# Renumbering the rows of a partition-wise DFT so that row and weight transfers get other partitions, and reloading a weight from a laid-out copy

## The chip, the cores and the metric

The kernel runs on one core of one Trainium2 chip. The metric is the device time of that core for one execution, in microseconds (us). A profile records one execution; its span, from first to last instruction, is about 2 us shorter than the device time of the same execution. Engines: PE is TensorE, PEld its weight loads, DVE is VectorE, ACT is ScalarE, POOL is GpSimd, and SP or SPq is SyncE and its queue, which issues nearly all DMAs of this kernel. A "stage" below begins with the first matmul of a group of matmuls.

The runs are labelled fast or slow. On one core that label rests only on the distance to the fastest run of the same kernel (1.5%).

## The reference

The kernel computes the output and all gradients of one block: a spectral filter with a residual, then a token MLP with a residual, both behind a LayerNorm, in bf16.

```python
# S = 2048, D = 448, Df = 225, F = 1792; all inputs bf16
def A(x, w_r, w_i):                               # spectral filter
    X = rfft2(x.astype(float32), axes=(-2, -1))   # [S, 225] complex
    X = X * (w_r + 1j * w_i)                      # w_r, w_i: [2048, 225]
    return irfft2(X, s=(S, D)).astype(bfloat16)
def B(x, w1, b1, w2, b2):                         # token MLP
    u = gelu(einsum("bsd,sf->bdf", layernorm(x), w1) + b1)
    return (einsum("bdf,fs->bds", u, w2) + b2).transpose(0, 2, 1)
h = x + A(layernorm(x), w_r, w_i)
y = h + B(layernorm(h), w1, b1, w2, b2)
# outputs: y and the gradients of x, w_r, w_i, w1, b1, w2, b2 for grad_out   (cut)
```

## The kernel before

The FFT over S = 2048 is written as matrix products with generated sine and cosine matrices, in two steps of 128 and 16. Between the steps a matmul result (one value of `s1`, 128 partitions) becomes eight partitions of 16 rows in another tile, which a DMA does. I call these the *row DMAs*: 16 per direction in the forward pass and again in the backward pass, each moving 128 packets of 904 bytes.

```python
def s1_stage(s1, ab):
    p1 = ps_ff(); p1v = ...
    nc.tensor.matmul(p1v, lhsT=Rm[:], rhs=ab, start=True, stop=True)
    cs = r452_ring.next(); evac(out=cs, in_=p1v)
    nc.sync.dma_start(out=D2[s1:P:16, :, 0:2, :], in_=cs)      # partitions s1, s1+16, ...
def s2_inv(g, y):
    ...                                                        # two matmuls with UTt, VTt
    ab = r452_ring.next(); evac(out=ab, in_=pv)
    nc.sync.dma_start(out=D3[g:P:16, :, :, :], in_=ab)
```

The spectral weight is brought into the matching order by 18 DMAs, each onto 16 neighbouring partitions with 15 or 16 rows (in two of them one row) of 450 bytes per partition. The same helper runs three times: the load for the forward pass, the same load again for the backward pass (into a buffer that holds MLP data until then), and the store of the weight's gradients.

```python
def w_io(Wv, dr, di, store, eng):
    for c_, d in ((0, dr), (1, di)):
        def go(part, g0, g1, d_ap):
            sb = Wv[part[0]:part[1], g0:g1, c_, 0:DF]
            ...                                   # eng.dma_start, in or out
        for f in range(4):
            go((16 * f, 16 * f + 16), 0, 16, d.rearrange("(a r) k -> a r k", r=P)[:, 16 * f:16 * f + 16, :])
        ...                                       # four mirrored groups, and one row group
...
w_io(W_view_F, A_w_r, A_w_i, False, nc.sync)      # before the s1 loop
...
nc.sync.dma_start_transpose(out=du_t..., in_=rD[...])
gp_.memset(W_view_B[:, :, :, DF:KW], 0.0)
w_io(W_view_B, A_w_r, A_w_i, False, nc.sync)      # backward, in rD
...
w_io(W_view_B, out_2, out_3, True, nc.sync)       # after the backward s2 stage
```

The second step of the FFT (the *s2 stage*) stores the forward spectrum for the backward pass and keeps two buffers for it (`X_ring`). Behind it stand two loads of 1 MB, the first chunks of w1; the second of them goes to a region shared with `D2`. And matmuls that do not depend on the stage at hand fill gaps of PE: in the forward s2 stage and before it, the MLP product of `grad_out` with w2, which needs *w2 transposes* (DMA transposes into `rE`); in the backward stages, the gradients of w2 (from `rE`) and w1 (from `rB`), both through transposes into `rst`.

```python
def fwd_mult(c2, xc):
    nc.sync.dma_start(out=xspec_d[:, 2 * c2:2 * c2 + 2, :, :], in_=xc)
    return w_mult(c2, xc, W_view_F, False)
s2_stage(fwd_mult, N_FILL_F[3], N_FILL_F[4])
w1c_ring = ring(r2, 0, 2, NT, 256)
w1cs = [load_w1c(0), load_w1c(1)]                 # 1 MB each
```

PE's instructions keep the order of the program (the kernel sets `manual_schedule` for PE alone). The compiler's scheduler orders all other engines, the SyncE queue included.

Of the kernel before, what the change touches and what calls it, by code (L numbers as in the profile page):

```python
# [16 lines left out]
P = 128  # L17
# [42 lines left out]
def kernel(  # L60
# [84 lines left out]
    cols = mem.tile([P, 48], F32, name="cols")  # L145
    _ci = [0]

    def col(n=1):
        i = _ci[0]
        _ci[0] += n  # L150
        assert _ci[0] <= 48
        return cols[:, i:i + n]
# [21 lines left out]
    smr = mem.tile([16, 2, P], BF16, name="smr")  # L174
    smc = mem.tile([P, 2, 16], BF16, name="smc")

    xspec_d = dram.tile([P, NG, 2, KW], BF16, name="xspec_d")
# [19 lines left out]
    gtail = mem.tile([16, P], BF16, name="gtail")  # L197
    gp_.memset(gtail[:], 0.0)
# [57 lines left out]
    def gen_R():  # L256
        ge = ftmp(2560, P)
        t = ftmp(2688, P)
        q = ftmp(2816, P)
        fr = ftmp(2944, P)  # L260
        ve.tensor_scalar(out=ge, in0=krow[:, 0:P], scalar1=65.0, scalar2=None, op0=ALU.is_ge)
        ve.scalar_tensor_tensor(out=fr, in0=ge, scalar=-64.0, in1=krow[:, 0:P], op0=ALU.mult, op1=ALU.add)
        ve.tensor_scalar(out=t, in0=fr, scalar1=pcol, scalar2=32.0, op0=ALU.mult, op1=ALU.add)
        ve.scalar_tensor_tensor(out=t, in0=ge, scalar=32.0, in1=t, op0=ALU.mult, op1=ALU.add)
        center(ve, q, t, 128)
        sc.activation(out=Rm[:], in_=q, func=ACT.Sin, scale=s128)
        gec = col()
        fc = col()
        oc = col()
        ve.tensor_scalar(out=gec, in0=pcol, scalar1=65.0, scalar2=None, op0=ALU.is_ge)  # L270
        ve.scalar_tensor_tensor(out=fc, in0=gec, scalar=-64.0, in1=pcol, op0=ALU.mult, op1=ALU.add)
        ve.tensor_scalar(out=oc, in0=gec, scalar1=32.0, scalar2=32.0, op0=ALU.mult, op1=ALU.add)
        t2 = ftmp(3072, P)
        q2 = ftmp(3200, P)
        ve.tensor_scalar(out=t2, in0=krow[:, 0:P], scalar1=fc, scalar2=oc, op0=ALU.mult, op1=ALU.add)
        center(ve, q2, t2, 128)
        sc.activation(out=RTm[:], in_=q2, func=ACT.Sin, scale=s128)

    c64, f2lo, lo, msk = col(), col(), col(), col(4)

    def gen_pidx(eng):
        w = col()
        floor_div(eng, c64, pcol, 64)
        floor_div(eng, w, pcol, 16)
        eng.tensor_scalar(out=lo, in0=w, scalar1=-16.0, scalar2=None, op0=ALU.mult)
        eng.tensor_tensor(out=lo, in0=lo, in1=pcol, op=ALU.add)
        eng.tensor_scalar(out=f2lo, in0=c64, scalar1=-4.0, scalar2=None, op0=ALU.mult)
        eng.tensor_tensor(out=f2lo, in0=f2lo, in1=w, op=ALU.add)
        for j in range(4):
            eng.tensor_scalar(out=msk[:, j:j + 1], in0=f2lo, scalar1=float(j), scalar2=None,  # L290
                              op0=ALU.is_equal)

    comp_ring = ring(rO, 0, 4, 32, 16)

    def expand(dst, q):
        d = dst[:].rearrange("p g (c f l) -> p (g c) f l", c=2, f=4)
        comp = comp_ring.next()
        sc.activation(out=comp, in_=q.rearrange("p g c l -> p (g c) l"), func=ACT.Sin, scale=s2048)
        for j in range(4):
            gp_.tensor_scalar(out=d[:, :, j, :], in0=comp, scalar1=msk[:, j:j + 1], scalar2=None, op0=ALU.mult)  # L300
        gp_.memset(dst[0:16, 0, 64:80], 0.0)
        gp_.memset(dst[64:80, 0, 0:16], 0.0)

    def gen_UV(eng):
        base = ftmp(512, 16, 2, 16)
        iota(base[:, :, 0, :], [[1, 16], [128, 16]])
        gp_.iota(base[:, :, 1, :], pattern=[[1, 16], [-128, 16]], base=1920, channel_multiplier=0,
                 allow_small_or_imprecise_dtypes=True)
        slf = col()
        eng.tensor_tensor(out=slf, in0=lo, in1=f2lo, op=ALU.mult)  # L310
        eng.tensor_scalar(out=slf, in0=slf, scalar1=16.0, scalar2=512.0, op0=ALU.mult, op1=ALU.add)
        ou, ov0, ov1, pu, pv, l64 = col(), col(), col(), col(), col(), col()
        eng.tensor_scalar(out=ou, in0=c64, scalar1=1536.0, scalar2=None, op0=ALU.mult)
        eng.tensor_tensor(out=ou, in0=ou, in1=slf, op=ALU.add)
        eng.tensor_scalar(out=ov0, in0=c64, scalar1=-512.0, scalar2=512.0, op0=ALU.mult, op1=ALU.add)
        eng.tensor_tensor(out=ov0, in0=ov0, in1=slf, op=ALU.add)
        eng.tensor_scalar(out=ov1, in0=ov0, scalar1=1024.0, scalar2=None, op0=ALU.add)
        eng.tensor_scalar(out=l64, in0=lo, scalar1=64.0, scalar2=None, op0=ALU.mult)
        for pt, o, k0 in ((pu, ou, -1536.0), (pv, ov1, -512.0)):
            eng.tensor_scalar(out=pt, in0=l64, scalar1=k0, scalar2=None, op0=ALU.add)  # L320
            eng.tensor_tensor(out=pt, in0=pt, in1=o, op=ALU.add)
        for dst, o0, o1, pt in ((Ut, ou, ou, pu), (Vt, ov0, ov1, pv)):
            t = ftmp(1024 if dst is Ut else 2048, 16, 2, 16)
            q = ftmp(1536 if dst is Ut else 2560, 16, 2, 16)
            for s_, o in ((0, o0), (1, o1)):
                eng.tensor_scalar(out=t[:, :, s_, :], in0=base[:, :, s_, :], scalar1=lo, scalar2=o,
                                  op0=ALU.mult, op1=ALU.add)
            eng.tensor_scalar(out=t[64:80, 0, 1, :], in0=base[64:80, 0, 0, :], scalar1=lo[64:80], scalar2=pt[64:80],
                              op0=ALU.mult, op1=ALU.add)
            center(eng, q, t, 2048)  # L330
            expand(dst, q)

    def gen_UVT(eng):
# [5 lines left out]
        v, v64 = col(), col()  # L339
        eng.tensor_scalar(out=v64, in0=lo, scalar1=128.0, scalar2=64.0, op0=ALU.mult, op1=ALU.add)  # L340
        eng.tensor_scalar(out=v, in0=lo, scalar1=-2.0, scalar2=15.0, op0=ALU.mult, op1=ALU.add)
        eng.tensor_tensor(out=v, in0=v, in1=c64, op=ALU.mult)
        eng.tensor_tensor(out=v, in0=v, in1=lo, op=ALU.add)
        eng.tensor_scalar(out=v, in0=v, scalar1=8.0, scalar2=None, op0=ALU.mult)
        eng.tensor_tensor(out=v, in0=v, in1=f2lo, op=ALU.add)
        eng.tensor_scalar(out=v, in0=v, scalar1=16.0, scalar2=None, op0=ALU.mult)
        t0 = ftmp(1024, 16, 2, 16)
        eng.tensor_scalar(out=t0, in0=srow, scalar1=v, scalar2=None, op0=ALU.mult)
        eng.tensor_tensor(out=base, in0=base, in1=t0, op=ALU.add)
        oc0, oc1 = col(), col()  # L350
        eng.tensor_scalar(out=oc0, in0=c64, scalar1=1024.0, scalar2=1024.0, op0=ALU.mult, op1=ALU.add)
        eng.tensor_scalar(out=oc1, in0=c64, scalar1=1024.0, scalar2=512.0, op0=ALU.mult, op1=ALU.add)
        for dst, o0, o1, pc in ((UTt, 512.0, 2048.0, 512.0), (VTt, oc0, oc1, 1024.0)):
            t = ftmp(1024 if dst is UTt else 2048, 16, 2, 16)
            q = ftmp(1536 if dst is UTt else 2560, 16, 2, 16)
            for c_, o in ((0, o0), (1, o1)):
                eng.tensor_scalar(out=t[:, :, c_, :], in0=base[:, :, c_, :], scalar1=o, scalar2=None, op0=ALU.add)
            eng.tensor_scalar(out=t[64:80, 0, 1, :], in0=srow[64:80, 0, 1, :], scalar1=v64[64:80], scalar2=pc,
                              op0=ALU.mult, op1=ALU.add)
            center(eng, q, t, 2048)  # L360
            expand(dst, q)
# [25 lines left out]
    gen_R()  # L387
# [5 lines left out]
    def w_io(Wv, dr, di, store, eng):  # L393
        for c_, d in ((0, dr), (1, di)):
            def go(part, g0, g1, d_ap):
                sb = Wv[part[0]:part[1], g0:g1, c_, 0:DF]
# [4 lines left out]
            for f in range(4):  # L401
                go((16 * f, 16 * f + 16), 0, 16,
                   d.rearrange("(a r) k -> a r k", r=P)[:, 16 * f:16 * f + 16, :])
            for f in range(4):
                g0 = 1 if f == 0 else 0
                first = P - 16 * f - g0
                go((64 + 16 * f, 80 + 16 * f), g0, 16,
                   bass.AP(d.tensor, d.offset + first * DF, [[P * DF, 16], [-DF, 16 - g0], [1, DF]]))
            go((64, 80), 0, 1, d.rearrange("(a r) k -> a r k", r=P)[:, 64:65, :])
# [14 lines left out]
    def resh_eng():  # L424
        _ei[0] += 1
        return nc.sync

# [25 lines left out]
    def s1_stage(s1, ab):  # L453
# [5 lines left out]
        nc.sync.dma_start(out=D2[s1:P:16, :, 0:2, :], in_=cs)  # L459
# [39 lines left out]
    def s2_inv(g, y):  # L499
# [6 lines left out]
        nc.sync.dma_start(out=D3[g:P:16, :, :, :], in_=ab)  # L506
# [83 lines left out]
    gen_pidx(ve)  # L590
    gen_UV(ve)
# [4 lines left out]
    w_io(W_view_F, A_w_r, A_w_i, False, nc.sync)  # L596
    fill(N_FILL_F[0])
    ab = None
    for s1 in range(NT):
# [4 lines left out]
        fill(N_FILL_F[1])  # L604
        if s1 % 2 == 1 and s1 // 2 + 3 < NT // 2:
            prep_x(s1 // 2 + 3)
        if s1 == 3:
            gen_UVT(ve)
# [8 lines left out]

    s2_stage(fwd_mult, N_FILL_F[3], N_FILL_F[4])
# [35 lines left out]
    gp_.memset(smr[:], 0.0)  # L654
# [68 lines left out]
    nc.sync.dma_start_transpose(out=goT[:, 3, S - 16:S], in_=gtail[:])  # L723
# [95 lines left out]
    gp_.memset(W_view_B[:, :, :, DF:KW], 0.0)  # L819
    w_io(W_view_B, A_w_r, A_w_i, False, nc.sync)  # L820
# [76 lines left out]
    w_io(W_view_B, out_2, out_3, True, nc.sync)  # L897
# [41 lines left out]
```

## Time and profile before

The kernel took 502.93 us (median of 3 runs, 500.79 to 504.31); the profiled span is 500.2 us.

| reading | before | view |
|---|---|---|
| PE, VectorE, ScalarE busy | 75%, 52%, 47% | page, busy shares |
| time of the DMA queue's packets over 16 engines | 81.9% of the span | page, DMA queues |
| PE's wait at the first w2-gradient matmul | 17.2 us | waits |
| PE's wait for w2 transposes at the start | 21.6 us | waits |
| DMA share, 20 to 80 us | 1.04 | stretches |

The page of the kernel before says which engines are busy (busy us, share of the span, instructions), how full the DMA engines are (packets, MB, share of 16 engines), and who holds the chain of waits that ended last:

```profile
PE 376.9 (75%) x1920; PEld 189.9 (38%) x1920; DVE 261.1 (52%) x709; ACT 235.1 (47%) x478; POOL 39.5 (8%) x50
...
q1 hardware_dynamic: 177320, 87.50, 81.9%
...
PE 40%; DMA 32%; DVE 17%; ACT 5%; SPq 4%; issue 3%; DVEq 0%; POOLq 0%; POOL 0%; ACTq 0%
```

No engine is busy throughout, so what is saved in a stage must be read from that stage. The view of PE's waits (engine, line, tile, releaser: us in all, times, longest us) has these among its largest in the kernel before:

```profile
PE ps_mm L567 <- DMA rE<-in_B_w_dram: 21.6, 3, 8.6
...
PE ps_mm L865 <- DMA rst<-rE: 17.2, 1, 17.2
...
PE ps_mm L880 <- DMA rst<-rB: 6.2, 2, 4.2
PE ps_ff L514 <- DMA r_73<-r_78: 5.5, 2, 3.7
```

L567 is the fill product behind the w2 transposes; L865 and L880 are the gradients of w2 and w1; L514 is the first matmul after the forward s2 stage, which needs the last row DMA. The reason for the 17.2 us stands in the timeline of the SyncE queue in the kernel before (start, time spent issuing, operation, out<-in, number):

```profile
324.20 1.26 SPq L437 DMA_TRANSPOSE rT<-rF  x1
...
326.48 4.70 SPq L400 DMA_DIRECT2D rD<-in_A_w_r_dram  x9
332.25 9.55 SPq L400 DMA_DIRECT2D rD<-in_A_w_i_dram  x9
342.88 0.62 SPq L459 DMA_DIRECT2D r_72<-r_78  x1
344.13 1.22 SPq L851 DMA_TRANSPOSE rst<-rE  x1
```

Eighteen issues of the second weight load hold the queue from 326.5 to 341.8 us, and the row DMA and the transpose that PE needs come behind them. What that does to PE is in the table by stretches of the kernel before (start:end, length, busy us and instructions of PE, PEld, DVE, ACT and POOL, granted TensorE clock, DMA share, GB/s; the DMA share adds up overlapping packets and may pass 1):

```profile
20.00:80.00 60.00, 40.07 (x197) 21.40 (x197) 38.62 (x119) 27.62 (x53) 30.76 (x28) 0.83 1.04 150
320.00:340.00 20.00, 9.36 (x35) 4.07 (x33) 0.00 (x0) 6.50 (x13) 0.25 (x1) 0.74 1.20 154
340.00:360.00 20.00, 8.67 (x28) 3.41 (x29) 1.31 (x4) 2.15 (x4) 0.00 (x0) 0.58 1.23 149
```

In all three the DMA engines are full (shares of 1.04, 1.20 and 1.23), though they move only 149 to 154 GB/s.

### The profile page before, as it was taken

The numbers are of one execution on the slowest core, as the hardware profiler recorded it, in microseconds if no ns is written. First come the engines' busy times: TensorE is split into PE (matmuls) and PEld (weight loads), VectorE is DVE, ScalarE is ACT, GpSimd is POOL, SyncE is SP. The second block draws the span as 40 slices with busy tenths as digits, with TensorE's granted clock in tenths as the row PEclk, the third lists the DMA queues.
The fourth block names the chain that finished last, engine by engine and source line by source line (L and its number), as shares of the span: only waits on it lengthen the run. The fifth ranks groups of instructions, "written<-read, shape, count | busy, mean of one in ns | idle before, by whom it ended". The sixth has DMA issues, their size and how long they took to land.

```text
span 500.2 us, 6019 instructions
## 1 busy us (share of the span) xinstructions
PE 376.9 (75%) x1920; PEld 189.9 (38%) x1920; DVE 261.1 (52%) x709; ACT 235.1 (47%) x478; POOL 39.5 (8%) x50
## 2 busy tenths in 40 slices
PE   2553865967798999639789999750899996969960
PEld 0221532433453445314344555320344443535530
DVE  9988362652494888602127867200137770235664
ACT  0622753653374545102222444730378784758771
POOL 6007960000000000000000000000000000000000
PEclk9975988899898999959999999965799998889995
DMA  9999799498975753785659999899956887976641
GB/s 234 209 156 158 149 152 168 119 221 173 269 215 188 196 171 85 159 220 160 191 164 169 202 168 192 163 140 94 194 188 190 215 202 181 166 197 183 205 166 55
DMA packets 177351, 87.87 MB, mean 176 GB/s; under 512 B 123433, under 2 KB 172585, under 8 KB 177193
## 3 DMA queue, kind: packets, MB, share of 16 engines
q1 hardware_dynamic: 177320, 87.50, 81.9%
q8 instruction: 15, 0.25, 0.2%
q14 instruction: 16, 0.12, 0.1%
HBM read 29.40 MB, written 23.89 MB: 107 GB/s over the span
## 4 chain that ended last, share of the span: by engine, by line
PE 40%; DMA 32%; DVE 17%; ACT 5%; SPq 4%; issue 3%; DVEq 0%; POOLq 0%; POOL 0%; ACTq 0%
DMA out_dram<-r_81 9%; PE ps_mm L865 8%; PE ps_mm L687 7%; PE ps_mm L809 5%; PE ps_mm L567 5%; PE ps_mm L880 4%; DVE stats L547 3%; PE ps_mm L732 3%; DMA r_73<-r_78 3%; DMA r_73<-in_B_w_dram 2%; DMA rC<-rD 2%; DMA rD<-in_A_w_i_dram 2%; DMA rE<-in_B_w_dram 2%; DMA xspec_d<-rS 2%; DVE r_81 L783 2%
## 5 line engine op out<-in xcount | busy, mean ns | idle before, releaser
L567 PE MATMUL ps_mm<-rC,rE 128*128 128x448 bf16 x224 | 62.5, 414 | 29.1 <-DMA rE<-in_B_w_dram 21.6
L865 PE MATMUL ps_mm<-rG,rst 112*128 112x512 bf16 x224 | 56.2, 400 | 17.9 <-DMA rst<-rE 17.2
L880 PE MATMUL ps_mm<-rC,rst 112*128 112x512 bf16 (+1 forms) x256 | 55.9, 367 | 6.9 <-DMA rst<-rB 6.2
L732 PE MATMUL ps_mm<-rE,rS 128*128 128x448 bf16 x224 | 44.9, 361 | 17.7 <-DMA rS<-in_B_w_dram 17.7
L687 PE MATMUL ps_mm<-rB,r_72 128*128 128x448 bf16 x224 | 45.0, 362 | 2.9 <-DVE rB L646 1.9
L567 PEld LDWEIGHTS <-rE 128*128 128x128 bf16 x224 | 24.3, 111 | 54.8 <-DMA rE<-in_B_w_dram 22.5
L809 PE MATMUL ps_mm<-rD,r_73 128*128 128x448 bf16 x224 | 43.7, 352 | 1.5 <-DMA r_73<-in_B_w_dram 1.5
L868 ACT CAST rO<-ps_mm 128x512 bf16<-128x512 f32 x56 | 31.7, 596 | 26.8 <-PE ps_mm L865 26.5
L865 PEld LDWEIGHTS <-rst 112*128 112x128 bf16 x224 | 22.8, 102 | 46.9 <-DMA rst<-rE 17.7
L732 PEld LDWEIGHTS <-rS 128*128 128x128 bf16 x224 | 21.9, 100 | 40.5 <-DMA rS<-in_B_w_dram 19.9
L883 ACT CAST rO<-ps_mm 128x512 bf16<-128x512 f32 (+1 forms) x60 | 30.1, 541 | 13.7 <-PE ps_mm L880 13.4
L880 PEld LDWEIGHTS <-rst 112*128 112x128 bf16 x256 | 25.0, 101 | 30.2 <-DMA rst<-rB 6.8
L744 ACT ACTIVATE r_81<-rC 128x448 bf16<-128x448 bf16 x16 | 9.2, 576 | 48.8 <-DVE r_81 L739 38.1
L687 PEld LDWEIGHTS <-r_72 128*128 128x128 bf16 x224 | 22.2, 100 | 25.5 <-issue 5.0
L528 PE MATMUL ps_ff<-csI,rAT 113*128 113x448 bf16 x128 | 30.7, 365 | 0.6 <-ACT rAT L517 0.5
L809 PEld LDWEIGHTS <-r_73 128*128 128x128 bf16 x224 | 21.6, 98 | 24.0 <-DMA r_73<-in_B_w_dram 2.6
L739 DVE SCALAR_TENSOR_TENSOR r_81<-ps_mm,b2col,r_81 128x448 bf16<-128x448 f32 x16 | 10.8, 682 | 37.9 <-PE ps_mm L732 37.8
L463 DVE TENSOR_SCALAR r_72<-r_72 128x904 bf16<-128x904 bf16 x8 | 2.6, 390 | 50.3 <-DMA r_72<-r_78 50.3
L450 ACT CAST r_78<-ps_ff 128x452 bf16<-128x452 f32 x32 | 17.2, 541 | 22.5 <-PE ps_ff L447 22.4
L517 ACT CAST rAT<-ps_ff 113x512 bf16<-113x512 f32 x32 | 18.4, 584 | 14.1 <-PE ps_ff L514 14.0
L477 ACT CAST rS<-ps_ff 128x452 bf16<-128x452 f32 x30 | 16.2, 542 | 15.2 <-PE ps_ff L476 10.6
L777 ACT ACTIVATE r_81<-ps_mm 128x448 bf16<-128x448 f32 x16 | 8.7, 543 | 29.8 <-PE ps_mm L809 28.7
(192 smaller groups left out, 599.6 us busy)
## 6 DMA issues: line engine op xcount, KB each, us to landing
r_72<-in_B_w_dram SPq DMA_DIRECT2D x7, 1024.0 KB
rS<-in_B_w_dram SPq DMA_DIRECT2D x8, 896.0 KB
out_dram<-rO SPq DMA_DIRECT2D x14, 512.0 KB
out_dram<-rO SPq DMA_DIRECT2D x16, 448.0 KB
r_72<-r_78 SPq DMA_DIRECT2D x32, 113.0 KB
r_73<-r_78 SPq DMA_DIRECT2D x32, 113.0 KB
out_dram<-r_81 SPq DMA_DIRECT2D x32, 112.0 KB
xspec_d<-rS SPq DMA_DIRECT2D x8, 226.0 KB
```

The costliest lines, as they stand in the source:

```text
L450: sc.copy(out=ab, in_=pv)
L477: evac(out=xc[:, i, :, :], in_=pv)
L517: sc.copy(out=aT[0:KC].rearrange("p a b -> p (a b)"), in_=pa[0:KC, :])
L528: nc.tensor.matmul(py[:, 0:D], lhsT=aT[0:KC, i, :], rhs=csI[0:KC, i // 2, i % 2, :], start=(i == 0), stop=(i == 3))
L567: nc.tensor.matmul(pg[:, 0:D], lhsT=wT[:, t, :], rhs=go_tp[:, t, :], start=(t == 0), stop=(t == NT - 1))
L687: nc.tensor.matmul(pu[:, 0:D], lhsT=w1c[:, t, jj * P:(jj + 1) * P], rhs=hln[:, t, :, :], start=(t == 0), stop=(t == NT - 1))
L732: nc.tensor.matmul(py[:, 0:D], lhsT=w2cs[t // 2][:, j, (t % 2) * P:(t % 2 + 1) * P], rhs=g_[:, j, :, :], start=(j == 0), stop=(j == NFB - 1))
L809: nc.tensor.matmul(pdh[:, 0:D], lhsT=wT[:, j, :], rhs=du[:, j, :, :], start=(j == 0), stop=(j == NFB - 1))
L865: nc.tensor.matmul(pw[:], lhsT=gt[0:DC, k, :], rhs=goT[0:DC, k, c * 512:(c + 1) * 512], start=(k == 0), stop=(k == 3))
L868: evac(out=o[:, c * 512:(c + 1) * 512], in_=pw[:])
L880: nc.tensor.matmul(pw[:, 0:n * P], lhsT=ht[0:DC, k, :], rhs=du_t[0:DC, 4 * c:4 * c + n, k, :], start=(k == 0), stop=(k == 3))
L883: evac(out=o[:, c * 512:c * 512 + n * P], in_=pw[:, 0:n * P])
```

## The change

The intent is to make the row DMAs and the weight transfers faster by giving them other partitions, and to make the second load of the weight cheap. There are four parts.

1. The rows of both FFT steps get other partition numbers. Row `s` used to lie on partitions s, s+16, s+32, ...; now it lies on a+0, a+4, ..., a+28 with a = 32*(s//4) + s%4. The generated matrices are rewritten for that order.
2. The weight follows: each of its 18 DMAs now goes to every eighth partition, and its issues are interleaved with the first loop, two per step, instead of standing ahead of it.
3. The weight in its laid-out form is stored once to DRAM (1.8 MB, contiguous), and the backward pass loads that copy with one DMA.
4. Two small buffers move, to make room.

```diff
+    w_d = dram.tile([P, NG, 2, KW], BF16, name="w_d")
...
+    def rowbase(s_):
+        return 32 * (s_ // 4) + s_ % 4
...
-        nc.sync.dma_start(out=D2[s1:P:16, :, 0:2, :], in_=cs)
+        nc.sync.dma_start(out=D2[rowbase(s1):rowbase(s1) + 29:4, :, 0:2, :], in_=cs)
...
-        nc.sync.dma_start(out=D3[g:P:16, :, :, :], in_=ab)
+        nc.sync.dma_start(out=D3[rowbase(g):rowbase(g) + 29:4, :, :, :], in_=ab)
...
-                sb = Wv[part[0]:part[1], g0:g1, c_, 0:DF]
+                sb = Wv[part:P:8, g0:g1, c_, 0:DF]          # and a yield after each pair
...
-    w_io(W_view_F, A_w_r, A_w_i, False, nc.sync)
+    w_loads = w_io(W_view_F, A_w_r, A_w_i, False, nc.sync)
...
+        next(w_loads, None)                                 # in the s1 loop
+        next(w_loads, None)
...
+    nc.sync.dma_start(out=w_d[:], in_=W_view_F)
     s2_stage(fwd_mult, N_FILL_F[3], N_FILL_F[4])
...
-    gp_.memset(W_view_B[:, :, :, DF:KW], 0.0)
-    w_io(W_view_B, A_w_r, A_w_i, False, nc.sync)
+    nc.sync.dma_start(out=W_view_B, in_=w_d[:])
...
-        d = dst[:].rearrange("p g (c f l) -> p (g c) f l", c=2, f=4)
-            gp_.tensor_scalar(out=d[:, :, j, :], in0=comp, scalar1=msk[:, j:j + 1], ...)
+            d = dst[:].rearrange("p g (lc f) -> p (g lc) f", f=4)       # for Ut and Vt
+                gp_.tensor_scalar(out=d[:, :, j], in0=comp, scalar1=msk[:, j:j + 1], ...)
(cut: the decoding of partition numbers, and the rest of the generation of Ut, Vt, UTt, VTt, RTm)
```

GpSimd writes each column block of `Ut` and `Vt` in four masked parts; a part used to be runs of 16 neighbouring elements and is now every fourth element.

## The prediction

> **What bounds the kernel now.** No single engine: the page has TensorE (PE) busy 75% of 500.2 us, VectorE 52%, the dynamic DMA queue 81.9% of 16 engines; the chain of waits is 40% PE, 32% DMA, 17% VectorE. By stage:
>
> - 0-85 us (spectral forward, first half): DMA-bound. Table by stretches: DMA share 0.94 to 1.23 until 80 us; PE has some 35 us of work there. The first weight load (18 DMAs) is issued at 14-37 us, ahead of w2 transposes for which PE waits 21.6 us.
> - 315-351: second weight load. Timeline of the SyncE queue: 18 issues fill 326.5-341.8; the row DMAs and the transpose that PE needs come behind. PE idles 17.2 us (view of waits), then runs 28 matmuls in 8.9 us instead of 6.0 at a granted clock of 0.58.
> - 426-441: 11 stores of weight gradients fill the queue for 8.35 us; the next transpose is 5.9 us on the chain.
> - 137-200, 263-315, 360-420: PE-bound.
>
> **What the change does.** Trace packets grouped by size: 450 B (weights) 12,288 at 75 ns mean (80 in the first load), 57.3 us of all 16 engines; 904 B (rows) 8,192 at 66 ns, 33.9 us; 14,336 B (the one contiguous 1.8 MB store) 543 ns, 4.4 us.
>
> [...] Estimates:
> [...]
> [...]
> - second load one copy of 14,464-byte rows: 20.9 -> about 5 us, one issue for 18;
> - added: that copy's store, 4.4 us near 80-90 us; some 30 small VectorE operations (60-65 ns each, 2 us).
>
> **On the chain.**
> - Start: less DMA time, w2 transposes no longer behind the weights, less the VectorE work: -8 us (-3 to -13).
> - 85-137: rows faster, but the store may delay the spectrum stores: 0 (-3 to +3).
> - Rows beside PE-bound 263-315: -1.
> - Second load: PE's wait 17.2 -> about 2, slow clock after it gone (-3): -17 (-13 to -20).
> - Gradient stores: -4 (-1 to -7).
> Sum -30.
>
> **Prediction: 473 us**, 8 times in 10 between 460 and 486. Faster by over 2%: 0.93; within: 0.06; slower: 0.01.
>
> **What would show each step.** 904-byte packets at 35-45 ns; 450-byte ones at 40-55, 8,192 of them; one weight load on rD of 5-6 us; PE's wait for the first transposes of the w2-gradient stage (17.2 us) under 5, granted clock near 1 behind it; the s2 matmuls, now from 85.9 us, starting at 73-82; a shorter wait for the transposes behind the gradient stores.
>
> **What would make it wrong.** The order outside PE is chosen by the compiler's scheduler: another queue order can put the new store ahead of row DMAs or transposes. VectorE, 94% busy until 20 us, may set the start: then it gains 0-3. [...] Transposes (153 us of engine time) may fill DMA time that comes free.

The sum came to -30 us (-8, 0, -1, -17 and -4). The 20.9 us that the text gives for the packets of the second load are low: in the trace before they took 24.3 us of 16 engines (4,096 at 95 ns). In the stretches that it calls PE-bound, PE was busy for 59.2 of 63, 49.3 of 52 and 56.9 of 60 us.

## The result and the profile after

The changed kernel took 482.46 us (median of 4 runs, 478.12 to 485.89) against 502.3 us of the kernel before in the same rounds: a ratio of 0.9574, with a 95% interval of 0.9497 to 0.9651. Ratios are the mean time of one kernel's fast runs over that of the other's fast runs of the same rounds, so they are not quite the ratio of the medians. The profiled span is 479.7 us.

The same lines of the page, of the kernel after:

```profile
PE 376.4 (78%) x1920; PEld 190.3 (40%) x1920; DVE 263.4 (55%) x732; ACT 235.0 (49%) x478; POOL 48.5 (10%) x50
...
q1 hardware_dynamic: 173224, 89.36, 76.0%
...
PE 38%; DMA 27%; DVE 18%; SPq 6%; ACT 4%; POOL 3%; issue 3%; DVEq 0%; ACTq 0%; POOLq 0%
```

PE's work is the same (376.9 and 376.4 us). The DMA part of the chain fell from about 160 us (32% of 500.2) to about 130 us (27% of 479.7). That this equals the predicted gain of 30 us is a coincidence, since the prediction was not made of chain shares. Two parts grew: the SyncE queue from about 20 to 29 us, and GpSimd from nothing to about 14 us. (These rest on percentages rounded by the page, so they are rough.) PE's waits in the kernel after:

```profile
PE ps_ff L480 <- DMA rT<-rF: 17.6, 5, 5.1
...
PE ps_mm L603 <- DMA rE<-in_B_w_dram: 8.0, 1, 8.0
PE ps_mm L918 <- DMA rst<-rB: 6.3, 1, 6.3
...
PE ps_ff L550 <- DMA r_73<-r_78: 5.4, 1, 5.4
PE ps_mm L903 <- DMA rst<-rE: 4.2, 1, 4.2
```

The wait of the w2 gradient fell from 17.2 to 4.2 us. The waits for w2 transposes fell from 21.6 to 8.0, but the wait for the transposes of x in the same stretch grew (L480, `rT<-rF`: 12.8 us of the 17.6 fall into the first 130 us, where it was 5.9 before; the rest is backward). The wait for `rst<-rB`, where the gradient stores stand, did not move (6.2 and 6.3). The timeline of the SyncE queue in the kernel after, at the second weight load:

```profile
321.00 1.25 SPq L473 DMA_TRANSPOSE rT<-rF  x1
322.96 0.34 SPq L858 DMA_DIRECT2D rD<-w_d  x1
...
323.87 0.64 SPq L495 DMA_DIRECT2D r_72<-r_78  x1
324.62 1.35 SPq L889 DMA_TRANSPOSE rst<-rE  x1
```

One issue of 0.34 us stands where eighteen stood, and the needed transpose goes out 3.6 us after the preceding one instead of 19.9 us after it (324.62 - 321.00 against 344.13 - 324.20). The table by stretches of the kernel after:

```profile
20.00:80.00 60.00, 40.74 (x201) 21.73 (x199) 42.60 (x143) 28.56 (x56) 39.66 (x28) 0.84 0.85 173
320.00:340.00 20.00, 11.60 (x43) 5.12 (x44) 1.31 (x4) 6.33 (x12) 0.00 (x0) 0.83 1.05 262
340.00:360.00 20.00, 20.00 (x97) 9.20 (x95) 7.93 (x17) 15.96 (x30) 0.00 (x0) 1.00 0.55 181
```

From 340 us PE runs without a gap at a granted clock of 1.00, where it was 8.67 us busy at 0.58 before. At the start (20 to 80 us) the DMA engines went from full to 0.85, and POOL from 30.76 to 39.66 us. So something there is no longer DMA-bound, and GpSimd does more.

To see where time went, I cut each run at the first matmul of each stage in its trace. The lengths are in us, and the five add up to the span; "control" is the changed kernel run once more, in another job.

| stage | before | after | after - before | control |
|---|---|---|---|---|
| start, up to the s2 stage | 85.9 | 78.8 | -7.1 | 78.9 |
| s2 stage | 41.7 | 45.8 | +4.1 | 44.8 |
| inverse, MLP and its input gradient | 185.9 | 185.6 | -0.3 | 187.0 |
| w2 gradient, with the backward FFT | 88.6 | 72.8 | -15.8 | 73.5 |
| w1 gradient, to the end | 98.1 | 96.7 | -1.4 | 94.9 |
| span | 500.2 | 479.7 | -20.5 | 479.1 |

And the packets of the DMA queue, grouped by size by my own count from the trace (mean ns of a packet):

| packets | before | after |
|---|---|---|
| 904 B, row DMAs, 8,192 | 66 ns | 53 ns (first step 55, second 50) |
| 450 B, first weight load, 4,096 | 80 | 33 |
| 450 B, second weight load, 4,096 | 95 | none |
| 450 B, gradient store, 4,096 | 49 | 55 (49 in the control) |
| 14,464 B, copy, stored and loaded, 128 each | none | 553 store, 742 load (4.4 and 5.9 us of 16 engines) |
| all packets, us of 16 engines | 412 | 366 |

So the prediction of the size was right to within its range (473 predicted, 460 to 486, and 482 measured), but a third of the expected gain of 30 us is missing. The experiments ask where it went.

### The profile page after: what moved, and what is told of

The parts are those of the page before. It is cut to its first block, busy times and chain, and to the rows that moved or that the text cites. A ratio compares the mean times of both kernels' runs of the same rounds, so it can differ in the third digit from the quotient of the medians.

```text
span 479.7 us, 6024 instructions
## 1 busy us (share of the span) xinstructions
PE 376.4 (78%) x1920; PEld 190.3 (40%) x1920; DVE 263.4 (55%) x732; ACT 235.0 (49%) x478; POOL 48.5 (10%) x50
## 4 chain that ended last, share of the span: by engine, by line
PE 38%; DMA 27%; DVE 18%; SPq 6%; ACT 4%; POOL 3%; issue 3%; DVEq 0%; ACTq 0%; POOLq 0%
DMA out_dram<-r_81 10%; PE ps_mm L903 8%; PE ps_mm L726 7%; PE ps_mm L848 6%; PE ps_mm L771 3%; PE ps_mm L918 3%; DMA xspec_d<-rS 3%; DVE stats L583 3%; PE ps_mm L603 3%; DMA r_73<-in_B_w_dram 2%; DMA out_dram<-rD 2%; POOL Ut L351 2%; DMA rst<-rE 2%; DVE r_81 L822 2%; SPq L857 2%
## 5 line engine op out<-in xcount | busy, mean ns | idle before, releaser
L603 PE MATMUL ps_mm<-rC,rE 128*128 128x448 bf16 x224 | 60.2, 403 | 14.2 <-DMA rE<-in_B_w_dram 8.0
L771 PE MATMUL ps_mm<-rE,rS 128*128 128x448 bf16 x224 | 45.2, 362 | 17.2 <-DMA rS<-in_B_w_dram 17.2
L903 PE MATMUL ps_mm<-rG,rst 112*128 112x512 bf16 x224 | 53.9, 390 | 4.2 <-DMA rst<-rE 4.2
L603 PEld LDWEIGHTS <-rE 128*128 128x128 bf16 x224 | 24.1, 110 | 42.0 <-issue 20.9
L906 ACT CAST rO<-ps_mm 128x512 bf16<-128x512 f32 x56 | 32.0, 594 | 13.0 <-PE ps_mm L903 12.8
L778 DVE SCALAR_TENSOR_TENSOR r_81<-ps_mm,b2col,r_81 128x448 bf16<-128x448 f32 x16 | 10.8, 682 | 38.1 <-PE ps_mm L771 38.0
L480 PE MATMUL ps_ff<-csF,rT 113*128 113x226 bf16 x64 | 13.0, 289 | 17.6 <-DMA rT<-rF 17.6
L513 ACT CAST rS<-ps_ff 128x452 bf16<-128x452 f32 x29 | 15.7, 540 | 15.1 <-DMA xspec_d<-rS 7.7
```

What stands on the lines that cost most here:

```text
L513: evac(out=xc[:, i, :, :], in_=pv)
L603: nc.tensor.matmul(pg[:, 0:D], lhsT=wT[:, t, :], rhs=go_tp[:, t, :], start=(t == 0), stop=(t == NT - 1))
L771: nc.tensor.matmul(py[:, 0:D], lhsT=w2cs[t // 2][:, j, (t % 2) * P:(t % 2 + 1) * P], rhs=g_[:, j, :, :], start=(j == 0), stop=(j == NFB - 1))
L903: nc.tensor.matmul(pw[:], lhsT=gt[0:DC, k, :], rhs=goT[0:DC, k, c * 512:(c + 1) * 512], start=(k == 0), stop=(k == 3))
L906: evac(out=o[:, c * 512:(c + 1) * 512], in_=pw[:])
```

## The experiments

My theory was that the new partitions explain the start and the load (faster packets) and that queue time explains the second load (one issue for 18). The open places were these: which part carries the gain, what made the s2 stage 4 us longer (the rival causes were the new store, the spectrum's buffers, and another queue order), whether GpSimd's masked writes limit the start, and what the gradient stores cost. Twelve kernels ran in three jobs, each on one chip and with its own runs of the kernel before. The medians of the kernel before were 500.98, 500.29 and 500.59 us.

### Control: the changed kernel once more

> The changed kernel once more, unedited, as the reference of the three that follow: 480 to 484 us, ratio to the kernel before 0.957 to 0.965; from first forward s2 matmul to first inverse matmul 44.5 to 46.5 us.

Measured: 478.68 us against 500.59, ratio 0.9578 (0.9533 to 0.9623). The ratio repeats the first result (0.9574), though the median lies just under the 480 to 484 us that I had expected; the medians differ by 4 us from chip to chip, so everything below is compared by ratio or within one job. The s2 stage was 44.8 us long here, and the w2 gradient stage 73.5 us.

### The copy alone

This is the kernel before with only part 3 of the change.

```diff
+    w_d = dram.tile([P, NG, 2, KW], BF16, name="w_d")
+    nc.sync.dma_start(out=w_d[:], in_=W_view_F)
     s2_stage(fwd_mult, ...)
...
-    w_io(W_view_B, A_w_r, A_w_i, False, nc.sync)
+    nc.sync.dma_start(out=W_view_B, in_=w_d[:])
```

> The kernel before, with only the laid-out DRAM copy: one store of it ahead of the forward s2 stage, one contiguous second load; old row numbering, weights still loaded first. Theory (the copy is worth some 16 us at the second load, and its store costs some 4 us in the forward s2 stage): PE's wait for the first transposes of the w2-gradient stage falls from 17.2 us to 4 or 5, s2 matmuls still start near 86 us, total 488 to 492. Rival ([...]in the changed kernel the second load is short also because rows and loads behind it are faster): wait stays over 9 us, total above 494.

Measured: 488.43 us against 500.98. The ratio of the runs labelled fast is 0.9667 (0.9587 to 0.9747), but it is pulled down by one execution of 480.89 us, beside which four of the others count as slow; the ratio of the medians is 0.975. PE's waits between 310 and 360 us in this run contain

```profile
PE ps_mm L866 <- DMA rst<-rE: 3.6, 1, 3.6
```

so the copy alone takes the wait of 17.2 us down to 3.6. The s2 stage was 42.3 us long, against 41.7 before. This says nothing about the store's effect on that stage: the scheduler issued the store at 49.1 us, and its packets ran from 50.4 to 55.8 us, long before the stage began. It began at 89.2 us instead of the expected 86 (85.9 before); these are single profiles, and whether the early store caused the delay is not shown.

### Everything but the copy

```diff
-    nc.sync.dma_start(out=w_d[:], in_=W_view_F)
...
-    nc.sync.dma_start(out=W_view_B, in_=w_d[:])
+    gp_.memset(W_view_B[:, :, :, DF:KW], 0.0)
+    for _ in w_io(W_view_B, A_w_r, A_w_i, False, nc.sync): pass      # 18 spread DMAs
```

> The changed kernel without the copy: both weight loads are the 18 renumbered DMAs[...], no store of the copy. Theory (18 issues at some 0.6 us set the pace of the second load once packets are at 33 to 36 ns): the wait at the second load is 10 to 13 us, against 4.2 with the copy and 17.2 before; the forward s2 stage (first s2 matmul to first inverse matmul) is 41 to 43 us instead of 45.8; total 484 to 489. Rival[...]: wait under 6 us, total at or under 480.

(The rival put the whole cost of the second load down to the times of its packets and none to its issues.)

Measured: 482.56 us against 500.98, ratio 0.9637 (0.9602 to 0.9672). PE's waits between 310 and 360 us:

```profile
PE ps_mm L903 <- DMA rst<-rE: 8.5, 1, 8.5
```

The renumbered load took 30 ns per packet and left half of the wait that the old one caused (I had expected 10 to 13 us of wait and a total of 484 to 489, so both came out lower). So once the rows are renumbered, the copy is worth only about 3 us by the ratios (0.9637 against 0.9578, and the two intervals overlap), although it is worth about 12.5 us by itself. The two halves of the change serve the same wait, and their gains don't add: about 18 and 12.5 us singly, about 21 together. And the s2 stage, without any store of the copy, was 45.3 us long where I had expected 41 to 43. This acquits the store. The runs with the gate and with the masked writes on VectorE, below, agree: in them the store's packets run in the first 7 us of the stage, which took 42.4 and 40.0 us.

### Rows back on the old partitions

Here only the row DMAs go to the old partitions, with everything else as in the changed kernel. The result is wrong (the weight gradients have a relative error of 1.4; the other outputs are within the usual error).

```diff
-        nc.sync.dma_start(out=D2[rowbase(s1):rowbase(s1) + 29:4, :, 0:2, :], in_=cs)
+        nc.sync.dma_start(out=D2[s1:P:16, :, 0:2, :], in_=cs)
-        nc.sync.dma_start(out=D3[rowbase(g):rowbase(g) + 29:4, :, :, :], in_=ab)
+        nc.sync.dma_start(out=D3[g:P:16, :, :, :], in_=ab)
```

> The changed kernel, but its row DMAs go to partitions s+16k again[...]; wrong numbers on purpose, all else kept. Theory[...]: 904-byte packets go from 50-55 ns back to 66-69, 7 us more of DMA time in the whole kernel, most of it off the chain: total 1 to 4 us longer. Rival (904-byte packets got faster because the queue is less crowded[...]): packets stay at 50-55 ns, total unchanged within 1 us.

Measured: 483.62 us against 500.98, ratio 0.9650 (0.9616 to 0.9683). The 904-byte packets went from 53 ns back to 66, the value before. That shows the partitions to be the cause of the packet time, and it shows how little they are worth: 3 to 4 us by the ratios (0.9650 against 0.9578 of the control, from two jobs whose intervals just overlap). The s2 stage began at 79.1 us, as in the control (78.9), and was as long (44.8).

### First weight load back on neighbouring partitions

```diff
-                sb = Wv[part:P:8, g0:g1, c_, 0:DF]
+                sb = Wv[part:P:8, ...] if store else Wv[16 * part:16 * part + 16, g0:g1, c_, 0:DF]
```

> The changed kernel, but each first-load DMA goes to 16 neighbouring partitions[...] again, in the new interleaved order; wrong numbers on purpose, the gradient stores stay renumbered. Theory (between 33 and 62 us the kernel waits for the SyncE queue's issues, 26.6 of 29 us, not for DMA engines): 450-byte load packets go from 33-36 ns to 66-80, 8 to 11 us more DMA time, but the s2 matmuls start at most 3 us later and the total grows by 0 to 4 us. Rival (the start is bound by the DMA engines, as the prediction said): s2 starts 7 to 10 us later, total grows by 6 to 10 us.

The result is wrong (the weight rows land on the wrong partitions; at this size of weight that hardly shows: the relative error is 0.0405). Measured: 485.85 us against 500.98, ratio 0.9704 (0.9659 to 0.9748). The load's packets took 64 ns, the row packets issued while the load ran (20 to 72 us) 115 on the mean against 54 in the kernel after, and single transposes of w2 held the SyncE queue for 5.7 to 7.7 us. PE's longest wait in the first 130 us (12.8 us in all in the kernel after):

```profile
PE ps_ff L480 <- DMA rT<-rF: 22.7, 5, 8.4
...
```

The s2 stage began at 91.6 us, 12.8 us later than in the changed kernel. My theory for the start, that it is bound by the time to issue DMAs and would lose at most 3 us, fell; the rival was right, and even too modest. In the new, interleaved order the spread of the *load* is what makes the start faster, far more than the spread of the rows. (Without it the start is 5.7 us longer than in the kernel before, so interleaving alone would not have helped; the spread load in the old place, ahead of the loop, was not run.) The end was only about 6 us later (by the ratio), because the s2 stage of this run was 38.5 us long instead of 45.8. That was the first hint at the cause of its length: in this run the scheduler had put a 1 MB load behind the last row DMAs.

### Masked writes on VectorE

```diff
             for j in range(4):
-                gp_.tensor_scalar(out=d[:, :, j], in0=comp, scalar1=msk[:, j:j + 1], ...)
+                eng.tensor_scalar(out=d[:, :, j], in0=comp, scalar1=msk[:, j:j + 1], ...)   # eng is VectorE
```

> The changed kernel, with the eight masked writes that build Ut and Vt on VectorE instead of GpSimd (2.5 us each there, with a step of four elements; 1.7 in the kernel before). Theory (GpSimd, busy 38 of the 40 us before 80, holds up the VectorE work queued behind its iota, and that holds ScalarE's evictions): VectorE's wait of 5.1 us at 50-55 us goes, the s2 matmuls start 2 to 5 us earlier; total 0 to 3 us shorter. Rival (GpSimd has slack; the transposes and rows in the SyncE queue set the pace): s2 starts within 1.5 us of 78.8, total unchanged.

The view of one line gives minimum, median and maximum ns, first and last start in us, and the shapes. The kernel before, the kernel after (both on GpSimd), and this run (on VectorE):

```profile
L300 POOL TENSOR_SCALAR Ut<-rO,cols x4: 1673/1733/1973, 40.6 to 45.7; 128x512 bf16<-128x512 bf16 x4
```

```profile
L351 POOL TENSOR_SCALAR Ut<-rO,cols x4: 2280/2652/2837, 44.3 to 51.9; 128x512 bf16<-128x512 bf16 x4
...
L393 POOL TENSOR_SCALAR UTt<-rO,cols x4: 1559/1561/1832, 67.4 to 72.3; 128x512 bf16<-128x512 bf16 x4
```

```profile
L351 DVE TENSOR_SCALAR Ut<-rO,cols x4: 777/780/795, 42.7 to 44.4; 128x512 bf16<-128x512 bf16 x4
```

With a step of four elements the same 128x512 write took GpSimd 2.65 us instead of 1.73 (for `Vt` 2.62 instead of 1.56); `UTt`, which keeps runs of 16 elements, still took 1.56. A busier VectorE beside it is not the reason for `Ut`: VectorE was busy for 57% of the time of these writes after, and for 97% before. The cost travels: in the kernel after, VectorE waits for GpSimd to reach the next index pattern, as its timeline shows in brackets (idle before, releaser):

```profile
55.17 0.91 DVE L410 TENSOR_SCALAR r_73<-r_73,cols 128x448 f32<-128x448 f32 x2 [5.14 <-POOL r_73 L216]
```

Measured: 469.0 us against 500.29, ratio 0.9355 (0.931 to 0.94), against 0.9578 of the control: about 11 us. I had expected at most 3. Of these, 4 us are the earlier start of the s2 stage (74.9 instead of 78.8 us), which the edit explains. The s2 stage itself was 40.0 us long, because the scheduler, with other timings, again put the 1 MB load behind the last rows. An edit in one place changed the order of the queue in another; that part of the gain is not the masked writes' own.

### Four spectrum buffers

In the s2 stage ACT waits 7.7 us in all for the spectrum stores that free its two buffers. This run gives the forward stage four.

```diff
-    X_ring = ring(rS, 0, 2, 2, 2, KW)
+    X_rings = [ring(rS, 0, 4, 2, 2, KW), ring(rS, 0, 2, 2, 2, KW)]   # forward, backward
```

> The changed kernel, with four buffers instead of two for the forward spectrum (free memory of that stage), so that an eviction does not wait for the store of two pairs before. Theory (the forward s2 stage is a chain through the spectrum stores in the SyncE queue, and takes back a lead: 28.7% of the chain there is this store): ScalarE's wait of 7.7 us for the store goes, and the time from first s2 matmul to first inverse matmul falls from 45.8 to 37-42 us, total 3 to 7 us shorter. Rival (the stage is paced by the row DMAs and transposes in the same queue): the wait moves to those, the stage stays within 2 us, total unchanged.

Measured: 478.85 us against 500.29, ratio 0.9554 (0.9507 to 0.9601): no different from the changed kernel. ACT's wait was gone and the last matmul of the stage started at 108.2 instead of 115.2 us. Then PE stood still, as its waits between 75 and 135 us show:

```profile
PE ps_ff L551 <- DMA r<-r: 10.0, 1, 10.0
```

(`r<-r` are the row buffers; in these runs the page writes them without their numbers.) It waits for the last row DMAs, and these stand behind the second 1 MB load in the queue. The rival was right: the buffers are not what ends the stage.

### The 1 MB load gated behind the last rows

The timeline of the SyncE queue in the kernel before, and in the kernel after, around the end of the s2 stage (`r_72<-in_B_w_dram` is the second 1 MB load, `r_73<-r_78` are row DMAs):

```profile
115.21 3.68 SPq L187 DMA_TRANSPOSE rE<-in_B_w_dram  x1
...
119.56 2.71 SPq L506 DMA_DIRECT2D r_73<-r_78  x4
122.32 0.61 SPq L624 DMA_DIRECT2D r_72<-in_B_w_dram  x1
```

```profile
110.71 0.61 SPq L663 DMA_DIRECT2D r_72<-in_B_w_dram  x1
111.42 5.60 SPq L188 DMA_TRANSPOSE rE<-in_B_w_dram  x1
117.12 0.64 SPq L542 DMA_DIRECT2D r_73<-r_78  x1
...
118.36 2.77 SPq L542 DMA_DIRECT2D r_73<-r_78  x4
```

Before, the load goes out last. After, it goes out first, and the transpose and five row DMAs follow it; the transpose then holds the queue for 5.60 us. To put the load back without touching anything else, one VectorE instruction writes one column of the load's buffer from the last row's data, so that the load has to wait for it.

```diff
-    w1cs = [load_w1c(0), load_w1c(1)]
+    w1cs = [load_w1c(0)]
+    ve.tensor_scalar(out=r2[:, 4096:4097], in0=last_ab[-1][:, 0, 0:1], scalar1=0.0,
+                     scalar2=None, op0=ALU.mult)       # last_ab: the last row buffer of s2_inv
+    w1cs.append(load_w1c(1))
```

> The changed kernel, with one column of the buffer of the second 1 MB w1 load written by VectorE from the last row of the s2 stage, so that this load is issued after the last five row DMAs instead of before them and before the last w2 transpose; nothing else in the SyncE queue moves. Theory (in all runs so far where this load stands ahead of the last rows the s2 stage takes 44.8 to 46.1 us, in all where it stands behind them 38.5 to 42.3; the scheduler's order, not the new store, takes back the lead): the stage falls to 40 to 43 us, the total by 2.5 to 5 us. Rival (the order is a symptom of something else, an early start of the stage): the stage stays at 44 to 46 us, total unchanged within 1 us.

Measured: 473.16 us against 500.59, ratio 0.9457 (0.9409 to 0.9505), with the control at 478.68 and 0.9578 in the same job. The timeline of the same stretch of the SyncE queue in this run:

```profile
111.00 2.28 SPq L188 DMA_TRANSPOSE rE<-in_B_w_dram  x1
113.38 0.63 SPq L545 DMA_DIRECT2D r<-r  x1
...
114.61 2.76 SPq L545 DMA_DIRECT2D r<-r  x4
117.47 0.61 SPq L666 DMA_DIRECT2D r<-in_B_w_dram  x1
```

The transpose now holds the queue for 2.28 us. PE's wait for the last rows, first in the control and then in this run (75 to 135 us):

```profile
PE ps_ff L550 <- DMA r<-r: 4.5, 1, 4.5
```

```profile
PE ps_ff L553 <- DMA r<-r: 1.6, 1, 1.6
```

The s2 stage was 42.4 us long, against 44.8 in the control and 41.7 before. That shows the cause of the longer stage: the scheduler had moved a large load ahead of the last small transfers that PE needs. (That the load's packets are what made the transpose hold the queue longer fits the 2.28 us, but was not tested separately.) The medians fell by 5.5 us, the spans of the two profiled executions by 8.5. Of these the s2 stage accounts for 2.4 us, and the stretch from there to the w2 gradient for 4.5. In that stretch PE stood idle about as long as in the control (22.6 and 23.4 us), but was busy for 3.7 us less with the same matmuls. The table by stretches shows why, first of the control and then of this run:

```profile
120.00:143.00 23.00, 18.76 (x125) 11.33 (x126) 13.69 (x37) 11.59 (x21) 0.00 (x0) 0.85 0.87 226
```

```profile
120.00:143.00 23.00, 21.19 (x152) 12.49 (x153) 18.56 (x49) 14.19 (x25) 0.00 (x0) 1.00 1.03 260
```

In the control the clock fell to half at 121 us, during the longer wait, and stayed there for 6.8 us; in this run it did not. Over the whole stretch the clock records give 10.8 us of clock lost in the control and 6.8 us here. So most of the gain after the stage went together with a higher granted clock, as it did at the second weight load (0.58 before and 1.00 after the change, from 340 to 360 us). That the shorter wait is what kept the clock up fits both places, but was not tested by itself.

### The weight's first load issued by ScalarE

```diff
-    w_loads = w_io(W_view_F, A_w_r, A_w_i, False, nc.sync)
+    w_loads = w_io(W_view_F, A_w_r, A_w_i, False, nc.scalar)
```

> The changed kernel, with the first load's 18 DMAs issued from ScalarE's queue instead of SyncE's; same partitions, same bytes. Theory (from 33 to 62 us the SyncE queue's issues are what the forward phase waits for, 26.6 of 29 us, 9.6 of them for weight loads): PE's wait for the x transposes (12.8 us) shrinks by 5 or more and the s2 matmuls start 3 to 8 us earlier than 78.8 us; but by the x2 result most of it is taken back by the s2 stage, so the total falls by 1 to 4 us. Rival (the DMA engines themselves, whoever issues): s2 starts within 2 us of 78.8, total unchanged within 1 us, or longer because ScalarE loses issue time.

Measured: 474.12 us against 500.29, ratio 0.946 (0.9415 to 0.9506), about 5 us better than the changed kernel (4.6 by the medians, 5.9 by the ratios; 1 to 4 had been expected). Five of the six executions took 472.19 to 476.0 us. The sixth, and it was the profiled one, took 980.01 us.

In that execution the matmuls of the group of line 848 took 761 ns on the mean, against 352 in the kernel after, and one started every 459 ns instead of every 189 (medians). ScalarE's casts of `rO` (586 ns, 594 in the kernel after), VectorE's statistics (613 and 610) and the row packets (54 and 53) kept their times, so of these only PE was slow. The clock of 1.000 that is listed for this execution is no measurement: its trace holds no clock records at all, where that of the kernel after holds 26. A low TensorE clock is therefore not excluded, and not shown either. The slow execution did not come back in the one later kernel that issues from ScalarE as well. So this run has a time but no profile to explain it: whether the gain is the relief of SyncE or another queue order stays open.

### Gradient stores spread over the last stage

```diff
-    for _ in w_io(W_view_B, out_2, out_3, True, nc.sync):
-        pass
+    w_stores = w_io(W_view_B, out_2, out_3, True, nc.sync)
...
     def gx_consumer(t, py):                  # once per row group of the last stage
+        next(w_stores, None)
+        next(w_stores, None)
```

> The changed kernel, with the 18 weight-gradient stores issued two at a time between the rows of the last stage instead of in one burst. Theory (16 stores at 0.66 us are limited by issue[...], so the renumbering left them alone; the burst of 8.9 us holds up the next transposes, on which PE waits 6.3 us): PE's wait for the transposes of the w1-gradient stage falls from 6.3 us to under 2; total 3 to 6 us shorter. Rival (the stores' time is DMA time that has to be paid anywhere in this stage): wait moves to other DMAs, total unchanged within 1.5 us.

Measured: 476.6 us against 500.29, ratio 0.9476 (0.9419 to 0.9534). Two quick executions (470.44 and 472.75) pull this ratio; the other four lie between 476.57 and 477.63, so the gain over the changed kernel is between 2 us (medians against the control, on different chips) and 5 us. PE's waits between 365 and 480 us, in the control and in this run:

```profile
PE ps_mm L918 <- DMA rst<-rB: 6.5, 1, 6.5
PE ps_ff L550 <- DMA out_dram<-rD: 1.8, 1, 1.8
```

```profile
PE ps_ff L550 <- issue: 2.7, 1, 2.7
PE ps_mm L918 <- ACT rO L921: 1.9, 1, 1.9
```

The wait behind the stores disappears, but others take its place: 4.6 us are left of 8.3, and the last stage was only 1.5 us shorter (93.4 against 94.9). What the stores had cost was not their packets. Before and after the change, the 18 issues hold the SyncE queue for some 0.6 us each (medians 0.58 and 0.61 us), and 11 or 12 of them stand in one piece (8.35 and 8.92 us) ahead of a transpose that PE needs.

### Two combinations

The first combination has the VectorE writes, the spread stores and the four buffers. The second adds the gate and the load from ScalarE.

```diff
 (first)   masked writes on VectorE + w_stores in gx_consumer + X_rings
 (second)  the first + the gate on load_w1c(1) + w_io(W_view_F, ..., nc.scalar)
```

> All that helped, together: masked writes of Ut and Vt on VectorE (469.0 alone), gradient stores spread over the last stage (476.6 alone), four spectrum buffers (stage end of the s2 matmuls 7 us earlier, lost again to the queue's order; here the 1 MB load stands behind the rows by itself). If the three gains add: 469 - 5 - 3 = 461 us; 459 to 464. Rival (four buffers and the masked writes pay for the same wait): 464 to 466.

> As c3, with the first weight load issued from ScalarE's queue (474.1 alone, 6 to 8 us) and the 1 MB load held behind the rows. If the SyncE queue's issue time in 33-62 us is still what the start waits for: s2 matmuls start 3 to 6 us earlier than in c3, total 455 to 460. Rival (with the masked writes off GpSimd the start is paced by the DMA engines): within 2 us of c3. One of six executions of x7 took 980 us; whether that comes back is watched here.

Measured: the first took 467.15 us against 500.59, ratio 0.9333 (0.9274 to 0.9392), and missed its expectation by 3 us; it is hardly better than the VectorE writes alone (469.0), and so is its s2 stage (40.1 us against 40.0). PE again waits 8.6 us for the last rows at its end, although the second 1 MB load stands behind them here without a gate (issued at 111.83 us, the last rows from 109.00): what stands ahead of them is the last w2 transpose, which holds the queue from 103.99 to 108.29. So four buffers gain nothing that these runs show, and this time the load's place is not the reason. The second took 463.77 us (457.64 to 468.05), ratio 0.919 (0.9128 to 0.9253). That ratio leaves out three executions of 465.41 to 468.05 us that count as slow beside two very quick ones; by medians it is 0.926. Its s2 stage was 35.6 us long; the last w2 transpose was out at 101.9 us and PE waited 5.3 us. Which of its two additions did that is not separated. The median missed the expected 455 to 460 us, and the expectation that ScalarE's issues would bring the s2 stage 3 to 6 us forward failed: it began at 73.7 us instead of 75.4. SyncE still spent 26.1 of the 29 us between 33 and 62 us issuing (26.6 in the changed kernel), because the transposes took the room that the loads had left (those of w2 12.1 us of it, against 4.5).

The second combination gave a correct result, and it is the fastest kernel: 37 us below the kernel before and 15 us below the changed kernel of the same job.

## Why the prediction was right or wrong

The predicted time was 473 us, 460 to 486, and "faster by over 2%" had 0.93. Measured were 482.5 us, so the class and the range were right, and the gain was 20 us instead of 30. By its terms:

| term | predicted | measured (stage starts) | what the runs showed |
|---|---|---|---|
| start | -8 (-13 to -3) | -7.1 | right; carried by the spread of the weight load (undoing it: +12.8); 4 us more were lost to GpSimd |
| forward s2 stage | 0 (-3 to +3) | +4.1, control +3.1 | wrong: a 1 MB load moved ahead of the last rows |
| PE-bound stretch, rows beside it | -1 | -0.3, control +1.1 | about nothing, as expected |
| second load | -17 (-20 to -13) | -15.8, control -15.1 | right |
| gradient stores | -4 (-7 to -1) | -1.4, control -3.2 | inside the range, but not by its mechanism: the wait went from 6.2 to 6.3 |
| sum | -30 | -20.5 | |

**The second load** was right in cause and size. The wait fell from 17.2 to 4.2 us and the load's packets took 5.9 us of the engines, where 5 had been predicted. The granted clock behind it went to 1.00. What the prediction did not see is that either half of the change removes half or more of this wait: the copy alone leaves 3.6 us of it, spread loads without the copy 8.5.

**The start** was right in size. It rested on the step "less DMA time, w2 transposes no longer behind the weights", and the run with the load on neighbouring partitions confirms the first half of that. Its list of costs was incomplete. It counted 30 small VectorE operations and read over the masked writes, which stand in the diff with a new access pattern. They cost GpSimd about 1 us each and VectorE a wait of 5.1 us.

**The s2 stage** is the step that failed by most: "rows faster, but the store may delay the spectrum stores: 0". The suspect was wrong. Neither the store (stage 45.3 us with the store removed, 42.4 with the store and the gate) nor the spectrum's buffers (gone: no gain) made it longer. The load's place in the queue did (42.4 us with the gate). The prediction had named "another queue order" among the things that could go wrong, but for the new store and without a number.

**The gradient stores** stayed within their wide range, but the reason for a gain failed: the store was costed like the load, as packets of about 80 ns that the new partitions would make faster. The trace before already had these packets at 49 ns, so 80, the load's number, was the wrong one to start from. They went to 55 (49 in the control), and the wait is made by the issues on the SyncE queue, whose number the change leaves as it is. The prediction had read that correctly from the profile ("11 stores of weight gradients fill the queue for 8.35 us") and then costed packets instead.

**The packet times** were off in both directions: rows 53 ns and not 35 to 45, loads 33 and not 40 to 55. The trace before held a better estimate. Its 896-byte packets took 49 ns and its 14,336-byte ones 543, which makes about 36.8 ps per byte and 16 ns per packet. From that follow, as an estimate, 49 ns for 904 bytes and 33 ns for 450; 53 and 33 were measured on the new partitions. (The packets that the estimate is from go to or from DRAM; the rows go between two places in SBUF.) The prediction scaled 66 and 80 ns by an assumption about partitions alone, which no trace showed. It hardly mattered: putting the rows back cost 3 us.

**What stays open.** Why packets take longer on one set of partitions than on another (the runs show 66 and 53 ns for the rows and 64 and 33 for the load, but not the mechanism), why the ScalarE-issued load gains 5 us, what the 980 us execution was, and which addition shortened the s2 stage of the last kernel.

## What to carry to other kernels

Cost a DMA by what limits it in that place: its packets (a fixed part and a part per byte, estimated from packets of the same trace; here 16 ns and 36.8 ps per byte), or the time that its issues hold the queue in front of something that an engine needs. In the kernel after, nine in ten issues held the SyncE queue for 0.33 to 0.82 us (plain DMAs) or 1.2 to 4.2 us (transposes; the longest 8.9), and in the kernel before 18 issues filled it for 15.3 us while PE waited 17.2. Here fewer issues helped the second (one copy alone, 1 issue for 18: a wait of 3.6 us instead of 17.2), and other partitions helped the first (the first load, 64 to 33 ns with the same order of issues, and the rows, 66 to 53, but not the stores, 49 to 55 and 49). Two improvements of the same wait did not add (about 18 and 12.5 us singly, 21 together), and the wait that was left (3.6 us with the copy alone, 8.5 without it) told which one still counted. Where a scheduler orders the queue, compare the order in the queue before and after, ahead of any theory on bandwidth: here one large load in front of five small transfers took back 3 to 4 of some 24 us, and one dependency put it right.
